# Mixing slots: low halves ahead of angle reductions, one result and one low half ahead of the last flips

## The chip, the cores and the metric

The kernel runs on one core of a Trainium2 chip. Its time is the device time of one execution in microseconds (us). A core has five engines that run their own instruction streams and meet only at semaphores: TensorE (PE, matmuls), VectorE (DVE), ScalarE (ACT), GpSimd (POOL) and SyncE (SP); POOL and SP mostly issue DMAs here. Each engine takes its instructions strictly in the order in which the program lists them.

## The reference

For 8 batches of 448 tokens and 12 heads of 64 features:

```
scores = cap * tanh(q k^T / 8 / cap);  attn = softmax(scores);  x = attn v      # x: 448 tokens x 768 features
theta  = x w_theta;  zr = x cos(theta);  zi = x sin(theta)
y      = w_tok_r zr + w_tok_i zi                                                # mixes tokens
u      = x + y;      out = u + max(u w_ch, 0)
```

## The kernel before, in words

Features stand on the partitions: a batch has six *feature blocks* of 128 features, numbered 0 to 5, each 448 tokens wide. Attention runs in 24 *slots* of four heads, three slots a batch. The dense work of a batch (its angles `theta`, the token mixing, the channel product) is spread over the three slots in which the attention of a later batch is computed, so that TensorE always has matmuls.

The order of the instructions is written out by hand: `PARTS` holds three strings of words, one for each kind of slot, and `run` turns each word into instructions. Every engine takes its own instructions in the order in which the words stand. `PARTS[0]` (*angle slot*) makes the angles, `PARTS[1]` (*mixing slot*) mixes the tokens, `PARTS[2]` makes the channel product. Batches 1 to 6 of the dense work use these strings; the first and the last batch have strings of their own in `OTHER`. So there are six mixing slots that follow `PARTS[1]`; they are called slots 1 to 6 here and start near 205, 310, 415, 520, 625 and 730 us.

The words that matter:

- `d4 d5`: `reduce`, L533 and L534, on DVE: the angles of blocks 4 and 5 are brought into one turn. `sc2`: `sincos` for blocks 4 and 5, on ACT: an absolute value (L542), a table load, cosine (L543), sine (L544). `r4 r5`: `rotate`, L548, on DVE: the features times cosine and sine.
- `f2 f3`, `f4 f5`: `flip`, L556, on DVE: blocks are transposed in squares of 32. `D1`, `D2`: `carry`, L567: 16 DMAs, 8 issued by SP and 8 by POOL, that complete the transposition of a pair of blocks into a tile `t`. D1 carries blocks 2 and 3, D2 blocks 4 and 5.
- `h`, `l`, `M`: each feature block goes through the mixing in two halves, a (four chunks of 128 columns) and b (three). `h` (`z_high`, L577, ACT) rounds a half to the high part `zh`; `l` (`z_low`, L584, DVE) subtracts it for the low part `zl`; `M` (`mix`, L594 to L596, PE) multiplies: for each chunk `zh` by the high weights, `zh` by the low weights, `zl` by the high weights. So M needs `zh` at its first matmul and `zl` at its third. `h0a l0a M0a` read the tile `t` of D0, blocks 2 and 3 that of D1, blocks 4 and 5 that of D2.
- `m0` (`mix_out`, L602, DVE): the mixed block 0 is read from PSUM and added to the features. The PSUM bank that it frees is the bank of M2.
- `S`, `t`, `e`: scores of the next heads on PE (L322), their tanh (L353) and exponential (L366) on ACT. `I`: `invert`, L472 and L475 on DVE and four DMAs (L479) on SP: the inverse of the sums of the softmax.
- `Pb1`, `Pa1`: L278 and L279 on DVE, high and low parts of q and k.

An `h` of a later half writes over the `zh` part of an earlier half, so it waits until the `M` of that half has ended. Each of the large tiles that D, f and z use is one of ten rooms that are handed on in order.

Of the kernel before, what the change touches and what calls it, by code (L numbers as in the profile page):

```python
# [78 lines left out]
def softcap_attn_then_spectral_mix(ctx, tc, qk2, v, cap, w_theta, w_tok, w_ch, outT):  # L79
# [527 lines left out]
    def chan_out(b, m):  # L607
# [6 lines left out]
    FRONT = "S0 t0 q0 q1 W cV0 v w0 e0 S1 t1 Ra cV1 e1 w1 S2 t2 Rb I Vr^ e2 S3 t3 V0^ w2 e3 w3 N"  # L614
    PARTS = (
# [179 lines left out]
```

## Time and profile before

| what | us |
|---|---|
| median of 3 runs | 876.16 (874.89 to 877.24) |
| the profiled execution, its own time | 876.32 |
| its span (first to last instruction) | 874.3 |
| PE busy | 856.1 (98% of the span) |
| DVE busy | 715.9 (82%) |
| ACT busy | 592.7 (68%) |
| POOL busy | 116.8 (13%) |
| granted TensorE clock, tenths of full speed | 9 (90% or more) in each of the 40 slices |

"Idle before" is time in which an engine had nothing running because its next instruction waited; the name behind the arrow is what ended that wait. In a timeline the first column is the start from the span's begin, the second the duration; rows of equal instructions that follow each other are merged (x2 and so on). Of PE rows the ends are modelled, so starts are compared with starts.

### The profile page before, as it was taken

What the parts mean: (1) busy time and instruction counts of PE and PEld (TensorE: products, weight loads), DVE (VectorE), ACT (ScalarE), POOL (GpSimd) and SP (SyncE); (2) the same over time, 40 slices, a digit from 0 to 9 for tenths busy, and PEclk for the clock granted to TensorE, in tenths of its full rate; (3) what the DMA queues carried; (4) which work ended last, traced back from release to release, by engine and by line L of the source; (5) the groups of instructions that cost most, each with busy time, mean ns of one, the idle gap of its engine ahead of it and who ended that gap; (6) DMA issues with size and microseconds to landing.
All of it is one profiled execution on the core that took longest, in us unless ns stands there. A gap on an engine that the chain in (4) does not pass through costs nothing.

```text
span 874.3 us, 13299 instructions
## 1 busy us (share of the span) xinstructions
PE 856.1 (98%) x4756; PEld 644.2 (74%) x4756; DVE 715.9 (82%) x1160; ACT 592.7 (68%) x693; POOL 116.8 (13%) x240
## 2 busy tenths in 40 slices
PE   9999999999999999999999999999999999999997
PEld 4336686876877868778687786787777876879996
DVE  5988989999788897898987898868979789785741
ACT  7898977678845786648956499555986378824420
POOL 1120332103100021001210013000130003200300
PEclk9999999999999999999999999999999999999999
DMA  8685386633422343223332414133152222310501
GB/s 312 203 305 200 92 249 207 199 106 83 139 64 74 97 115 107 83 84 98 94 87 85 126 55 128 53 94 117 53 145 78 85 85 78 102 43 27 144 9 58
DMA packets 51691, 99.74 MB, mean 114 GB/s; under 512 B 11232, under 2 KB 42208, under 8 KB 51616
## 3 DMA queue, kind: packets, MB, share of 16 engines
q1 hardware_dynamic: 38880, 58.81, 22.1%
q0 software_dynamic: 9568, 29.89, 11.1%
q10 hardware_dynamic: 3168, 10.09, 3.7%
q8 instruction: 39, 0.64, 0.3%
q14 instruction: 36, 0.29, 0.1%
HBM read 54.72 MB, written 11.01 MB: 75 GB/s over the span
## 4 chain that ended last, share of the span: by engine, by line
PE 78%; DVE 11%; ACT 7%; issue 2%; SPq 1%; DMA 1%; DVEq 0%
PE s L322 11%; PE a L424 10%; PE mx L594 7%; PE ch L503 7%; PE mx L596 7%; PE mx L595 7%; PE ch L505 7%; PE ch L504 7%; PE th L503 4%; PE th L504 4%; PE th L505 4%; DVE z L548 2%; PE r L456 2%; DVE g_row L556 2%; PE a L418 1%
## 5 line engine op out<-in xcount | busy, mean ns | idle before, releaser
L353 ACT ACTIVATE p<-s,singles 128x1792 f32<-128x1792 f32 (+1 forms) x54 | 93.3, 1729 | 101.1 <-PE s L322 100.8
L567 POOL DMA_DIRECT2D t<-g_row x160 | 79.5, 504 | 546.1 <-DVE x_row L486 161.8
L594 PE MATMUL mx<-wtk_h,zh 128*128 128x448 f32 x336 | 124.6, 371 | 6.7 <-DVE x L602 3.3
L596 PE MATMUL mx<-wtk_h,zl 128*128 128x448 f32 x336 | 123.9, 369 | 4.0 <-DVE zl L584 4.0
L595 PE MATMUL mx<-wtk_l,zh 128*128 128x448 f32 x336 | 123.3, 367 | 0.0
L366 ACT ACTIVATE p<-p,singles 128x1792 f32<-128x1792 f32 (+1 forms) x76 | 118.2, 1556 | 1.3 <-PE a L424 0.6
L503 PE MATMUL ch<-us,wch_h 128*128 128x448 f32 x288 | 107.0, 371 | 0.0
L503 PE MATMUL th<-xs,wth_h 128*128 128x448 f32 x288 | 106.7, 370 | 0.0
L504 PE MATMUL th<-xs,wth_h 128*128 128x448 f32 x288 | 105.6, 367 | 0.0
L505 PE MATMUL th<-xs,wth_l 128*128 128x448 f32 x288 | 105.6, 367 | 0.0
L505 PE MATMUL ch<-us,wch_l 128*128 128x448 f32 x288 | 105.3, 366 | 0.0
L504 PE MATMUL ch<-us,wch_h 128*128 128x448 f32 x288 | 105.2, 365 | 0.0
L424 PE MATMUL a<-p,v 128*64 128x448 f32 x492 | 101.8, 545 | 0.0
L594 PEld LDWEIGHTS mx<-wtk_h,zh 128*128 128x128 f32 x336 | 63.1, 188 | 17.9 <-ACT zh L577 8.8
L584 DVE TENSOR_TENSOR zl<-t,zh 128x512 fp32r<-128x512 f32 x88 | 52.7, 616 | 28.3 <-ACT zh L577 19.8
L424 PEld LDWEIGHTS a<-p,v 128*64 128x64 f32 x492 | 32.9, 136 | 56.5 <-issue 50.4
L596 PEld LDWEIGHTS mx<-wtk_h,zl 128*128 128x128 f32 x336 | 63.1, 188 | 12.1 <-DVE zl L584 6.6
L577 ACT CAST zh<-t 128x512 fp32r<-128x512 f32 x88 | 47.2, 560 | 31.0 <-PE mx L595 16.6
L595 PEld LDWEIGHTS mx<-wtk_l,zh 128*128 128x128 f32 x336 | 63.1, 188 | 5.4
L503 PEld LDWEIGHTS th<-xs,wth_h 128*128 128x128 f32 x288 | 54.0, 188 | 9.5 <-issue 3.1
L503 PEld LDWEIGHTS ch<-us,wch_h 128*128 128x128 f32 x288 | 54.0, 187 | 8.3 <-DVE few L472 1.5
L504 PEld LDWEIGHTS th<-xs,wth_h 128*128 128x128 f32 x288 | 54.0, 187 | 5.0 <-DVE xs L496 0.2
(596 smaller groups left out, 1648.0 us busy)
## 6 DMA issues: line engine op xcount, KB each, us to landing
v<-in_v ACTq DMA_DIRECT2D x22, 448.0 KB, 3.2
q<-in_qk SPq DMA_DIRECT2D x40, 224.0 KB, 3.2
t<-g_row SPq DMA_DIRECT2D x160, 56.0 KB, 2.4
t<-g_row POOLq DMA_DIRECT2D x160, 56.0 KB, 2.1
out_dram<-x SPq DMA_DIRECT2D x39, 224.0 KB, 1.9
k<-in_qk SPq DMA_DIRECT2D x35, 224.0 KB, 3.5
bc<-ri SPq DMA_DIRECT2D x58, 112.0 KB, 2.4
x_row<-in_qk SPq DMA_DIRECT2D x21, 224.0 KB, 2.8
```

The source lines that it names most:

```text
L322: nc.tensor.matmul(out[h][:, :S], kk[rows], qq[rows], start=m == 0, stop=m == len(products) - 1)
L353: nc.scalar.activation(pp, t[:, :m, :, :S], AF.Tanh, scale=qscale)
L366: nc.scalar.activation(pp, pp, AF.Exp, scale=cap_sb)
L424: nc.tensor.matmul(acc_of["a", s, i][h * D : (h + 1) * D, :S], vt[s][:, 6 * i + 3 * h + c, :], U[s, (i, c)][:, h, :], start=first and c == ...
L503: nc.tensor.matmul(acc[:, :S], wh[:, j, ms], t[:, 0, :], start=j == 0, stop=False)
L504: nc.tensor.matmul(acc[:, :S], wh[:, j, ms], t[:, 1, :], start=False, stop=False)
L505: nc.tensor.matmul(acc[:, :S], wl[:, j, ms], t[:, 0, :], start=False, stop=j == NJ - 1)
L567: queue.dma_start(t[32 * m : 32 * m + 32, d * S : (d + 1) * S], f[32 * d : 32 * d + 32, m * S : (m + 1) * S])
L584: nc.vector.tensor_tensor(zl, tokens(b, j)[:, c0:c1], zh.bitcast(F32), op=ALU.subtract)
L594: nc.tensor.matmul(acc[:, :S], zh, wtk_h[:, c, :], start=c == 0, stop=False)
L595: nc.tensor.matmul(acc[:, :S], zh, wtk_l[:, c, :], start=False, stop=False)
L596: nc.tensor.matmul(acc[:, :S], zl, wtk_h[:, c, :], start=False, stop=c == NC2 - 1)
```

## The change

Two of the three strings change; no instruction is added or removed. In the diff, the first pair is the end of `PARTS[0]`, the second the beginning of `PARTS[1]`:

```diff
-        " e2 T3 y3 Pa0 Pb0 q1 e3 d3 a1a a1b F1 sc1 T4 y4 T5 y5 r2 r3 f2 f3 D1 d4 d5",
-        "S0 t0 V0 h0a l0a h0b l0b W h1a Ra Rb Vr cV0 cV1 sc2 Pa1 S1 Pb1 q0 M0a l1a r4 h1b t1 M0b r5 l1b I f4 f5 D2 e0 h2a M1a l2a e1 M1b m0 h2b l2b w1"
+        " e2 T3 y3 Pa0 Pb0 q1 e3 d3 a1a a1b F1 sc1 T4 y4 T5 y5 r2 r3 f2 f3 D1",
+        "S0 t0 V0 h0a l0a h0b l0b W h1a Ra Rb Vr cV0 cV1 d4 d5 sc2 Pa1 S1 Pb1 q0 M0a l1a r4 h1b t1 M0b r5 l1b h2a I m0 l2a f4 f5 D2 e0 M1a e1 M1b h2b l2b w1"
```

The first place is DVE at the beginning of slot 4. `z_2` and `z_4` are the angle tiles of blocks 2, 3 and of blocks 4, 5; `t_0` is the tile of D0. Before:

```order
L556 STREAM_TRANSPOSE g_row<-z_2_4624 128x7x4x32 x2
L533 SCALAR_TENSOR_TENSOR z_4_4718<-z_4_4718 128x448
L534 TENSOR_SCALAR z_4_4718<-z_4_4718 128x448
L533 SCALAR_TENSOR_TENSOR z_4_4718<-z_4_4718 128x448
L534 TENSOR_SCALAR z_4_4718<-z_4_4718 128x448
L584 TENSOR_TENSOR zl_4790<-t_0_4631,zh_4789 128x512
L584 TENSOR_TENSOR zl_4790<-t_0_4631,zh_4789 128x384
L278 CAST q35h<-q_4511 128x448
```

and now, in the same place:

```order
L556 STREAM_TRANSPOSE g_row<-z_2_4624 128x7x4x32 x2
L584 TENSOR_TENSOR zl_4786<-t_0_4631,zh_4785 128x512
L584 TENSOR_TENSOR zl_4786<-t_0_4631,zh_4785 128x384
L533 SCALAR_TENSOR_TENSOR z_4_4718<-z_4_4718 128x448
L534 TENSOR_SCALAR z_4_4718<-z_4_4718 128x448
L533 SCALAR_TENSOR_TENSOR z_4_4718<-z_4_4718 128x448
L534 TENSOR_SCALAR z_4_4718<-z_4_4718 128x448
L278 CAST q35h<-q_4511 128x448
```

The two low halves of block 0 (l0a, l0b) and the four reductions (d4, d5) have changed places; what stands ahead and behind is the same.

The second place is DVE later in the same slot, from l1b on; `mx_0` is the mixed block 0, `t_1` the tile of D1. Before:

```order
L584 TENSOR_TENSOR zl_4790<-t_0_4631,zh_4789 128x384
L472 RECIPROCAL few_4870<-r_4803 32x14 x4
L475 STREAM_TRANSPOSE ri_4869<-few_4870 128x448
L556 STREAM_TRANSPOSE g_row<-z_4_4718 128x7x4x32 x2
L584 TENSOR_TENSOR zl_4790<-t_1_4746,zh_4789 128x512
L602 TENSOR_TENSOR x_0_3530<-mx_0_4841,x_0_3530 128x448
L584 TENSOR_TENSOR zl_4790<-t_1_4746,zh_4789 128x384
```

and now:

```order
L584 TENSOR_TENSOR zl_4786<-t_0_4631,zh_4785 128x384
L472 RECIPROCAL few_4871<-r_4799 32x14 x4
L475 STREAM_TRANSPOSE ri_4870<-few_4871 128x448
L602 TENSOR_TENSOR x_0_3530<-mx_0_4841,x_0_3530 128x448
L584 TENSOR_TENSOR zl_4786<-t_1_4746,zh_4785 128x512
L556 STREAM_TRANSPOSE g_row<-z_4_4718 128x7x4x32 x2
L584 TENSOR_TENSOR zl_4786<-t_1_4746,zh_4785 128x384
```

The result read m0 and the low half l2a stand ahead of the two flips f4 and f5 now, where they stood behind them.

On ACT one instruction moves: the rounding h2a, which l2a needs. `s_1` are scores, `p_0` the softmax tile. Before:

```order
L577 CAST zh_4789<-t_0_4631 128x384
L353 ACT_TABLE_LOAD
L353 ACTIVATE g_row<-s_1_4821,singles 128x1792
L366 ACTIVATE p_0_4780<-p_0_4780,singles 128x1792
L577 CAST zh_4789<-t_1_4746 128x512
L366 ACTIVATE g_row<-g_row,singles 128x1792
```

and now:

```order
L577 CAST zh_4785<-t_0_4631 128x384
L353 ACT_TABLE_LOAD
L353 ACTIVATE g_row<-s_1_4821,singles 128x1792
L577 CAST zh_4785<-t_1_4746 128x512
L366 ACTIVATE p_0_4776<-p_0_4776,singles 128x1792
L366 ACTIVATE g_row<-g_row,singles 128x1792
```

h2a has gone ahead of the exponential e0. The matmuls, the DMAs of each queue and the rooms of the tiles keep their order.

## Rows read from the trace of the kernel before

**Rows 1.** Who waited for whom, PE: us in total, times, longest.
```profile
PE mx L596 <- DVE zl L584: 4.0, 6, 0.7
```

**Rows 2.** Timeline, PE: first matmul of M2 in slots 1 to 6.
```profile
227.54 0.44 PE L594 MATMUL mx<-wtk_h,zh 128*128 128x448 f32 x1 [1.10 <-ACT zh L577]
...
332.63 0.44 PE L594 MATMUL mx<-wtk_h,zh 128*128 128x448 f32 x1 [1.26 <-DVE x L602]
...
437.21 0.44 PE L594 MATMUL mx<-wtk_h,zh 128*128 128x448 f32 x1 [1.24 <-DVE x_row L602]
...
542.51 0.44 PE L594 MATMUL mx<-wtk_h,zh 128*128 128x448 f32 x1 [0.99 <-DVE x L602]
...
647.83 0.44 PE L594 MATMUL mx<-wtk_h,zh 128*128 128x448 f32 x1 [1.09 <-DVE x_row L602]
...
753.10 0.44 PE L594 MATMUL mx<-wtk_h,zh 128*128 128x448 f32 x1 [1.07 <-DVE x L602]
```

**Rows 3.** Timeline, PE, slot 4: M0 (three rows), M1b, M4a.
```profile
529.91 0.37 PE L595 MATMUL mx<-wtk_l,zh 128*128 128x448 f32 x1
530.97 0.47 PE L596 MATMUL mx<-wtk_h,zl 128*128 128x448 f32 x1 [0.69 <-DVE zl L584]
531.27 0.36 PE L594 MATMUL mx<-wtk_h,zh 128*128 128x448 f32 x1
...
537.88 0.37 PE L596 MATMUL mx<-wtk_h,zl 128*128 128x448 f32 x1
...
551.67 0.37 PE L596 MATMUL mx<-wtk_h,zl 128*128 128x448 f32 x1
```

**Rows 4.** Timeline, DVE, slot 4: l0a and l0b, Pb1, r4 and r5, l1b, f4 and f5, l2a, m0.
```profile
530.23 1.16 DVE L584 TENSOR_TENSOR zl<-t,zh 128x512 fp32r<-128x512 f32 x2
531.30 0.39 DVE L278 CAST q35h<-q 128x448 fp32r<-128x448 f32 x1
...
534.59 2.09 DVE L548 TENSOR_TENSOR z<-z,x 128x896 f32<-128x896 f32 x2 [0.78 <-ACT z L544]
536.60 0.55 DVE L584 TENSOR_TENSOR zl<-t,zh 128x384 fp32r<-128x384 f32 x1
...
539.03 2.11 DVE L556 STREAM_TRANSPOSE g_row<-z 128x896 f32<-128x896 f32 x2
541.05 0.65 DVE L584 TENSOR_TENSOR zl<-t,zh 128x512 fp32r<-128x512 f32 x1
541.74 0.62 DVE L602 TENSOR_TENSOR x<-mx,x 128x448 f32<-128x448 f32 x1
```

**Rows 5.** Timeline, ACT: h4a in slot 2; L542 of sc2 and h4a in slot 4.
```profile
339.71 0.62 ACT L577 CAST zh<-t 128x512 fp32r<-128x512 f32 x1 [1.97 <-DMA t<-g_row]
...
530.41 0.95 ACT L542 ACTIVATE z<-z 128x896 f32<-128x896 f32 x1 [1.29 <-DVE z L534]
...
548.55 0.62 ACT L577 CAST zh<-t 128x512 fp32r<-128x512 f32 x1 [0.93 <-PE mx L594]
```

**Rows 6.** Timeline, SP: the issues of D2 in slot 4.
```profile
541.77 5.00 SPq L567 DMA_DIRECT2D t<-g_row  x8
```

**Rows 7.** DMA issues: count, KB each, median us from issue to landing.
```profile
t<-g_row SPq DMA_DIRECT2D x160, 56.0 KB, 2.4
```

**Rows 8.** Timeline, DVE: l4a and l4b in slots 1 to 6.
```profile
234.69 1.16 DVE L584 TENSOR_TENSOR zl<-t,zh 128x512 fp32r<-128x512 f32 x2 [1.99 <-ACT zh L577]
...
340.36 1.16 DVE L584 TENSOR_TENSOR zl<-t,zh 128x512 fp32r<-128x512 f32 x2 [2.74 <-DMA k<-in_qk]
...
444.31 1.16 DVE L584 TENSOR_TENSOR zl<-t,zh 128x512 fp32r<-128x512 f32 x2 [2.11 <-ACT zh L577]
...
549.20 1.16 DVE L584 TENSOR_TENSOR zl<-t,zh 128x512 fp32r<-128x512 f32 x2 [1.68 <-DMA k<-in_qk]
...
656.09 1.16 DVE L584 TENSOR_TENSOR zl<-t,zh 128x512 fp32r<-128x512 f32 x2 [3.27 <-DMA k<-in_qk]
...
760.21 1.16 DVE L584 TENSOR_TENSOR zl<-t,zh 128x512 fp32r<-128x512 f32 x2 [2.10 <-ACT zh L577]
```

## The prediction

> **What bounds the kernel now.** I read the table of waits for PE first, then the PE timeline of a mixing slot, then DVE, ACT and SP in the same window, and last the same few instructions in all six mixing slots. PE is busy for nearly the whole span, so the end moves only by what TensorE waits. Outside the start, its named waits are two, each once in every mixing slot. The first is M0's third matmul, which needs the low half l0a: 4.0 us over six slots [rows 1]. The second is M2's first matmul, 0.99 to 1.26 us a slot, 6.75 us together [rows 2]: the bank that M2 needs is freed by m0 (in slot 1 the name given is the rounding of h2b, which ended at nearly the same time). Both are waits on DVE's order: l0a stands behind d4 and d5, m0 behind f4 and f5. What the reader should look for next is what else hangs on d5 and on f5, since the change makes these two later.
>
> **The change part by part, in slot 4.**
>
> *First low halves ahead of d4 and d5.* M0's second matmul starts at 529.91 and the mixing runs at 0.207 us a matmul (531.27 to 537.88 is 32 of them), so the third could start at 530.12; it starts at 530.97, and the one behind it 0.30 later and not 0.21 [rows 3]. Now l0a is done before PE asks for it, which gives 0.94 us. The price stands on DVE: l0a and l0b take from 530.23 to 531.30 [rows 4], so d5 ends 1.07 us later. ACT's absolute value had sat idle for 1.29 us and started when d5 ended [rows 5], so sc2 starts and ends 1.07 later; DVE in turn had sat idle for 0.78 us and started r4 when sc2's sine ended [rows 4]. So r4, r5 and l1b come 1.07 us later: nothing on the way has slack to hide it.
>
> *What l1b holds up.* l1b ends at 537.15 [rows 4]. From the start of l0a to the matmul that waited for it were 0.74 us, about 0.13 beyond the low half itself, so M1b's third matmul could start at 537.28; it starts at 537.88 [rows 3], a slack of 0.6. Now l1b allows it at 538.35, while PE, 0.94 early, arrives at 536.94. The wait of 0.7 at M0 is gone and one of 1.4 stands at M1b; with the slower restart (0.09) PE is 0.56 us behind its old time there.
>
> *m0, l2a (and h2a) ahead of f4 and f5.* m0 would start when I is done, 539.03 plus 1.07, and end near 540.7 [rows 4]. PE reaches M2 at 542.51 less 0.99 plus 0.56, 542.08 [rows 2], so M2's wait goes altogether. Up to here slot 4 has gained 0.43 us, and the six slots 6.75 less 3.36, 3.4 us. h2a ahead of e0 is free: the half that it writes over belongs to M0, long done by then, and e0's first reader on DVE stands behind the low halves of block 3; without that cover it would cost one rounding, 0.6 us a slot.
>
> *What is late next: D2.* f4 and f5 now stand behind m0 (0.62) and l2a (0.69, from 541.05 to 541.74) and behind an l1b that is 1.07 late: f5 ends 2.38 us later than at 541.14 [rows 4]. D2 starts 0.63 after f5; SP needs 5.00 us for its eight issues [rows 6], and the last lands 2.4 us behind its issue [rows 7]: 541.77 plus seven eighths of 5.00 plus 2.4 is 548.5, and h4a, the first reader of that tile, starts at 548.55 [rows 5]. The name at that row is a matmul that had long been done; in slot 2 the same wait is put down to the carry itself, 1.97 us [rows 5]. So h4a and l4a sit on the carry already before the change, and they move by the full 2.38.
>
> The Trainium skill has a rule against this step: "DMA: Bandwidth & Descriptors", section "Issuing engines are not separate DMA queues", says that the time in which a sequencer starts its DMAs is usually small beside the transfers themselves. The trace disagrees here: eight issues take 5.00 us and a landing 2.4. By the rule D2 would be there some 2.4 us after 541.77, block 4 would have 4 us to spare, and the sum would end at the 3.4 us gained; this is the second rival.
>
> *The sum.* M4a's third matmul comes 9.16 us after M2's first (551.67 less 542.51) [rows 2, 3]. Now it cannot start before l4a's old start plus 2.38 plus 0.74, and restarts 0.09 slower. Taking l4a from [rows 8] and M2 from [rows 2], the six slots end later by 1.20, 1.78, 1.15, 0.74, 2.31 and 1.16 us, 8.3 together. What was gained further up is in this already: it only makes the wait at M4 longer. Slots 2 and 5 stand out: there l4a came 7.73 and 8.26 us after M2, in the other four 7.01 on average. If what held up those two carries doesn't meet them again, 2.0 us less are lost, 6.4. No row says whether it does; I take 7.6, nearer to what the trace has. Behind M4 nothing else waits: l5a and l5b move with l4a. The profiled execution took 876.32 us, 0.16 over the median of the runs; 876.32 plus 7.6 less 0.2 is 883.8 against 876.16.
>
> Unknown costs: whether l0a, right behind the flip f3, starts as promptly as d4 did (0 to 0.1 us a slot, which would add up to 0.6); and whether D2's issues, 1.3 us further behind the four DMAs of I than before, run faster or meet other loads (0.5 us a slot either way). The forecast's own range is 880 to 886.5.
>
> **The rivals.**
>
> *Both waits go and nothing takes their place.* 6 times 0.94 and 6.75 are 12.4 us: 864. For it: the two waits are the only ones that PE shows, and each is moved. Against: it needs sc2 not to hang on d5 and h4a not on f5, and both rows say that they do.
>
> *D2 has slack (faster).* The carry is ready before block 4 needs it, and the slot keeps what it has at M2: 3.4 us less, 872.8. One mechanism: h4a's wait is the buffer that it writes over, as the row of slot 4 names it (a matmul, not the carry), and then it follows PE. It decides the sign from the point where carries land on average 1.4 us before h4a starts (2.38 less the mean slack of 0.99 that the sum contains). Against: the sum of issue and landing meets h4a's start to 0.1 us, and slot 2 names the carry.
>
> *sc2 is not delayed (no change).* If the absolute value could start 1.07 earlier than I think, f5 is late by 1.31 alone. Then the slots lose 0.13, 0.71, 0.08, -0.33, 1.24 and 0.09 us: 1.9, so 878. Against: the row's 1.29 us of idle end with d5.
>
> **How the numbers follow.** Forecast 0.75, both waits gone 0.05, D2 with slack 0.12, sc2 on time 0.08. A measurement of this kernel can tell about 0.3%, 2.6 us, from no change. The two rivals that gain lie beyond that: faster 0.17. Within 0.3%: the third rival and a small tail of the forecast, 0.11. Slower 0.72. The range for 8 in 10 takes the forecast's own range and reaches down over the third rival, and up for slots that all behave like slot 5: 876 to 887.
>
> **What would show it.** Right: M0's wait for `zl` and M2's for L602 gone in all six slots; a new wait of about 1.4 us of M1b's third matmul on DVE's `zl`; L542 on ACT still released by d5, 1.07 us later; D2's first issue about 2.4 us later against M0's start; and a wait of M4's first and third matmul on `zh` and `zl`, 0.7 to 2.5 us a slot, with h4a released by the carry. PE's idle time in the mixing grows from 10.7 to about 18 us. Wrong: no wait at M4 (then the second rival), no wait at M1b (then the first or third), or waits in the channel slots, where DVE's backlog of 2.4 us would first be felt.

## The result, and the profile after

The changed kernel takes 881.5 us (881.19 to 882.98, 4 runs) against 876.5 us (874.89 to 877.24, 4 runs) of the kernel before, measured beside it: a ratio of 1.0063, interval 1.0044 to 1.0081. It is slower by 5.0 us, with 883.8 forecast. The profiled execution took 881.24 us, its span is 879.5.

The table of waits of the kernel after, PE (us in total, times, longest), answers to [rows 1]:

```profile
PE mx L596 <- DVE zl L584: 8.7, 6, 1.5
PE mx L594 <- ACT zh L577: 1.9, 5, 0.7
```

The first line stands for one wait in each of the six slots, as before, but twice as dear. The second is new at the matmul where it stands now, and the three lines of M2's waits, 6.75 us in [rows 2], are gone. Which matmuls wait is read from the timeline of PE in slot 4 (start, duration, engine, line; in brackets the idle time before it and what ended it): M0's first and third matmul, M1b's third, M2's first, M4a's first and third, to be held against [rows 2, 3].

```profile
532.93 0.47 PE L594 MATMUL mx<-wtk_h,zh 128*128 128x448 f32 x1
...
533.43 0.36 PE L596 MATMUL mx<-wtk_h,zl 128*128 128x448 f32 x1
...
541.84 0.47 PE L596 MATMUL mx<-wtk_h,zl 128*128 128x448 f32 x1 [1.52 <-DVE zl L584]
...
545.47 0.47 PE L594 MATMUL mx<-wtk_h,zh 128*128 128x448 f32 x1
...
554.61 0.48 PE L594 MATMUL mx<-wtk_h,zh 128*128 128x448 f32 x1 [0.31 <-ACT zh L577]
...
555.34 0.47 PE L596 MATMUL mx<-wtk_h,zl 128*128 128x448 f32 x1
```

M0 and M2 start without a wait; M1b and M4a wait. Behind them, the timeline of DVE in slot 4: l0a and l0b, r4 and r5, l1b, m0, f4 and f5, l4a and l4b; to be held against [rows 4, 8].

```profile
531.86 1.16 DVE L584 TENSOR_TENSOR zl<-t,zh 128x512 fp32r<-128x512 f32 x2
...
539.23 2.10 DVE L548 TENSOR_TENSOR z<-z,x 128x896 f32<-128x896 f32 x2 [1.82 <-ACT z L544]
541.24 0.55 DVE L584 TENSOR_TENSOR zl<-t,zh 128x384 fp32r<-128x384 f32 x1
...
543.58 0.62 DVE L602 TENSOR_TENSOR x<-mx,x 128x448 f32<-128x448 f32 x1
...
544.72 2.10 DVE L556 STREAM_TRANSPOSE g_row<-z 128x896 f32<-128x896 f32 x2
...
554.59 1.16 DVE L584 TENSOR_TENSOR zl<-t,zh 128x512 fp32r<-128x512 f32 x2 [2.42 <-DMA k<-in_qk]
```

DVE's idle time before r4 grew from 0.78 to 1.82 us, about the time by which l0a and l0b were moved ahead. ACT's idle time before the absolute value grew by 1.31 us, from 1.29 to 2.60, and the carry now releases h4a in slot 1 (timeline of ACT: h4a of slot 1, the absolute value of sc2 in slot 4), against [rows 5]:

```profile
236.67 0.62 ACT L577 CAST zh<-t 128x512 fp32r<-128x512 f32 x1 [1.60 <-DMA t<-g_row]
...
535.04 0.95 ACT L542 ACTIVATE z<-z 128x896 f32<-128x896 f32 x1 [2.60 <-DVE z L534]
```

Both traces have 4,756 matmuls in one order, so that their starts can be subtracted one by one. By how much PE fell behind its old time at each place, in us over the six slots, beside what the prediction said (each step is counted up to the matmul behind the named one, so that its late restart is in it; a whole slot goes from M0's first matmul to the one behind M4a's third):

| place | predicted | measured |
|---|---|---|
| M0's third matmul | -5.6 | -5.6 |
| M1b's third | +9.0 | +10.5 |
| M2's first | -6.75 | -7.0 |
| M4a's first to third | +11.0 | +5.3 |
| a whole slot, slots 1 to 6 | 1.20, 1.78, 1.15, 0.74, 2.31, 1.16 | 0.53, 0.82, 0.66, 0.45, 0.99, 0.42 |
| the mixing slots together | +7.6 | +3.9 |
| the last matmul | +7.6 | +5.1 |

(Predicted: 0.94, 1.50 and M2's waits from the prediction's steps; M4 is what is left to 7.6.) The four places add up to 3.2 us, the other 0.7 lie between them. Of the 1.2 us between the last two rows, 0.94 are there at M0 of slot 1, ahead of the first changed instruction: 0.33 arise in the first 10 us and 0.6 in the twelve score matmuls near 72 us. The changed order has no part in them. The other 0.3 fall outside the measured stretches of the slots and stay open. The traces of the experiments stand 0.03 to 0.74 us behind the kernel before at that M0.

### The profile page after: what moved, and what is told of

Same layout as the page of the kernel before. It is cut to its first block, busy times and chain, and to the rows that moved or that the text cites. A ratio compares the mean times of both kernels' runs of the same rounds, so it can differ in the third digit from the quotient of the medians.

```text
span 879.5 us, 13287 instructions
## 1 busy us (share of the span) xinstructions
PE 861.6 (98%) x4756; PEld 643.9 (73%) x4756; DVE 716.7 (81%) x1160; ACT 592.2 (67%) x693; POOL 118.1 (13%) x240
## 4 chain that ended last, share of the span: by engine, by line
PE 86%; ACT 5%; SPq 4%; DMA 2%; issue 1%; DVE 1%; ACTq 0%; POOL 0%; POOLq 0%
PE a L424 13%; PE s L322 13%; PE th L503 7%; PE ch L503 7%; PE th L504 7%; PE th L505 7%; PE ch L505 7%; PE ch L504 7%; PE mx L596 5%; PE mx L594 5%; PE mx L595 5%; SPq L567 4%; PE a L418 2%; PE r L456 2%; DMA t<-g_row 2%
## 5 line engine op out<-in xcount | busy, mean ns | idle before, releaser
L567 POOL DMA_DIRECT2D t<-g_row x160 | 80.7, 516 | 551.6 <-DVE x_row L486 159.2
L503 PEld LDWEIGHTS th<-xs,wth_h 128*128 128x128 f32 x288 | 54.0, 188 | 9.6 <-issue 3.1
L505 PEld LDWEIGHTS ch<-us,wch_l 128*128 128x128 f32 x288 | 54.0, 188 | 4.9
```

The lines of the kernel that those rows point to most:

```text
L503: nc.tensor.matmul(acc[:, :S], wh[:, j, ms], t[:, 0, :], start=j == 0, stop=False)
L505: nc.tensor.matmul(acc[:, :S], wl[:, j, ms], t[:, 0, :], start=False, stop=j == NJ - 1)
L567: queue.dma_start(t[32 * m : 32 * m + 32, d * S : (d + 1) * S], f[32 * d : 32 * d + 32, m * S : (m + 1) * S])
```

## The experiments

Each was timed in five rounds beside the kernel before, whose median was 876.0, 875.8 and 875.7 us in the three groups, and 876.5 beside the changed kernel: a difference between runs of two groups is uncertain by up to 0.8 us. The words of the diffs are those of `PARTS`; of each string only the stretch that differs is shown.

### Each move alone

The first move alone (second half of the change undone):

```diff
-M0b r5 l1b h2a I m0 l2a f4 f5 D2 e0 M1a e1 M1b h2b l2b w1
+M0b r5 l1b I f4 f5 D2 e0 h2a M1a l2a e1 M1b m0 h2b l2b w1
```

> The first move alone: d4 and d5 behind l0a and l0b, the rest in the old order. My theory (d5 late makes sc2 late, sc2 makes r4, r5 and l1b late, f5 makes D2 late): M0's wait goes (-0.85 us a slot), M1b's third matmul waits 1.5 as in the changed kernel, m0 ends 1.07 later than before and M2's wait grows to about 1.5. D2's first issue follows f5 by about 0.6 again, since SP is still busy with I's four DMAs, and M4 does not wait, because PE is late itself. Net +1.2 a slot: 883.7 us (880.5 to 886). Rival (sc2 or l1b have slack and the first move is a gain that the second move loses): M0's wait goes and nothing comes for it, 871.5 us.

Measured: 883.65 us (883.42 to 885.05), ratio 1.0087 (1.0073 to 1.0101). Table of waits, PE:

```profile
PE mx L596 <- DVE zl L584: 8.6, 6, 1.5
PE mx L594 <- DVE x L602: 4.8, 3, 1.6
PE mx L594 <- DVE x_row L602: 3.2, 2, 1.6
PE mx L594 <- ACT zh L577: 1.5, 1, 1.5
```

The wait at M1b is the whole 8.6 us already, and M2 now waits 1.5 to 1.6 for m0 in all six slots (one of them put down to `zh`). The move that was to free M0 costs more than it frees. The rival is out by 12 us.

The second move alone (first half undone): `d4 d5` stand at the end of `PARTS[0]` again.

> The second move alone: h2a, m0 and l2a ahead of f4 and f5, d4 and d5 in their old place. My theory: M0's wait stays (0.69), no wait at M1b, M2's wait goes (-1.15 a slot), f5 ends 1.3 later but D2 starts only 0.8 later, and l4a 0.8 later takes back part of it at M4: -0.4, +0.2, -0.5, -0.9, +0.7, -0.4 us in the six slots, about -1.3 in all: 875 us (873 to 877.5). Rival (D2 has slack): the full gain at M2, 869.6 us.

Measured: 873.48 us (872.82 to 873.78), ratio 0.9968 (0.9956 to 0.998). PE's lag over a slot is -0.5, -0.2, -0.6, -0.8, +0.3 and -1.0 us. Table of waits, PE:

```profile
PE mx L596 <- DVE zl L584: 4.1, 6, 0.8
PE mx L594 <- ACT zh L577: 0.9, 2, 0.7
```

M2 gives back 7.0 us and M4 takes 3.3: PE comes to block 4 about 1 us earlier and the carry's first issue 0.2 to 1.25 us later, more than the slack that M4 had, and the gain is 2.5 us and not 7. Here the second move is a small gain. It is the first that makes the change slower.

### The chain from d5 to r4

```diff
-Vr cV0 cV1 d4 d5 sc2 Pa1 S1
+Vr cV0 cV1 G d4 d5 sc2 Pa1 S1
+            elif word == "G":
+                nc.scalar.activation(curve, quarter, AF.Sin)
```

`curve` is one column that nothing reads any more. The sine on it makes ACT load the table of sc2's cosine while it has nothing to do.

> The changed kernel with one more ACT instruction, a sine of one column ahead of the absolute value, so that the table load of sc2 (1.28 us) runs while ACT waits for d5. Nothing else moves. My theory (the chain from d5 over sc2 to r4 is what delays l1b and D2): r4 starts 1.28 earlier, M1b's wait falls from 1.5 to about 0.2, D2 starts 1.28 earlier and with it l4a, so M4 ends 1.28 earlier too: -7.7 us against the changed kernel, 873.8 us (872 to 876). Rival (l1b waits for something else, such as h1b or its place on DVE): M1b's wait stays, 881.5 us.

Measured: 873.93 us (872.51 to 875.06), ratio 0.9978 (0.9969 to 0.9987); 7.6 us less than the changed kernel. Timeline of ACT, slot 4, and the waits of PE:

```profile
528.34 1.28 ACT L711 ACT_TABLE_LOAD   x1
...
530.90 0.95 ACT L542 ACTIVATE z<-z 128x896 f32<-128x896 f32 x1 [1.07 <-DVE z L534]
531.89 1.05 ACT L543 ACTIVATE z<-z,singles 128x896 f32<-128x896 f32 x1
```

```profile
PE mx L594 <- ACT zh L577: 2.9, 6, 1.2
PE mx L596 <- DVE zl L584: 1.1, 4, 0.3
```

The cosine follows the absolute value at once, r4 comes 1.29 us earlier (5.01 us behind M0's first matmul in slot 4, 6.30 in the changed kernel), and the 8.7 us of M1b's waits have shrunk to 1.1 at most. The Trainium skill, "ScalarE: Activation LUTs", section "What ACT_TABLE_LOAD costs", gives some 2.66 us for a switch of tables, of which about 1.28 are the load and the rest a drain. Here the load alone counts, 1.28 us in its row and 1.29 in what its removal from the chain gives.

The same instruction in the kernel before:

> The kernel before with the one-column sine ahead of sc2's absolute value, nothing else. My theory: sc2 ends 1.28 earlier, r4 starts at once behind l1a, 0.78 earlier, and with it f4, f5, m0 and D2; M0's wait stays at 0.7, M2's falls from 1.1 to about 0.3, and M4, whose carry moves with it, does not wait: -0.78 a slot, 871.3 us (869.5 to 873). Rival (M2's wait hangs on the rounding h2a or on another bank, or DVE's idle time is not on the path): 876 us.

Measured: 870.1 us (870.02 to 871.07), ratio 0.9938 (0.9925 to 0.9952). The waits of PE for m0 fell to 0.7 and 0.2 us in all:

```profile
PE mx L596 <- DVE zl L584: 4.1, 6, 0.7
...
PE mx L594 <- DVE x L602: 0.7, 3, 0.4
...
PE mx L594 <- DVE x_row L602: 0.2, 1, 0.2
```

M4 did not wait, since its carry moved with PE. The gain is 1.0 us larger than forecast (5.7 us, not 4.7).

### The carry D2 and block 4

One more DVE instruction ahead of f4 in the changed kernel:

```diff
-h2a I m0 l2a f4 f5 D2
+h2a I m0 l2a l2a f4 f5 D2
```

> The changed kernel with the low half l2a computed twice (the second writes the same values), so that f4, f5 and D2 come one DVE instruction of 0.6 us later and nothing else does; M2's third matmul still finds l2a done. My theory (in the changed kernel block 4 sits on the carry D2 without slack in all six slots): M4's waits grow by 0.62 a slot, +3.7 us against the changed kernel: 885.2 us (884 to 886.5). Rival (M4's waits there are mostly PE's own, the carry has some slack): 881.5 us.

Measured: 886.52 us (884.75 to 886.69), ratio 1.0117 (1.0102 to 1.0133), 5.0 more than the changed kernel and 1.3 more than expected. PE's waits for `zh` at M4a:

```profile
PE mx L594 <- ACT zh L577: 7.2, 6, 1.5
```

They grew from 1.9 to 7.2 us; there is no slack. D2 came 0.70 to 0.82 us later and not 0.62. A further 1.2 us of the profiled run come from slot 2 alone, told below.

Two of POOL's eight DMAs of D2 given to SP, in the changed kernel:

```diff
-queue = nc.gpsimd if (b < B - 1 or i) and d >= 2 else nc.sync
+queue = nc.gpsimd if (b < B - 1 or i) and d >= 2 and not (i == 2 and 0 < b < B - 1 and d == 2 and m < 2) else nc.sync
```

> The changed kernel with two of the eight DMAs of D2 that POOL issues given to SP, which issues ten then and POOL six; the data are the same. My theory (the carry lands when SP has issued its last DMA, plus 2.4 us): SP's stretch grows from 5.0 to 6.2 us, the last landing and with it l4a come 1.24 later, +7.4 us in six slots: 889 us (887 to 890.5). Rival (the transfers themselves set the landing, and issue time is small beside them): 881.5 us.

Measured: 889.57 us (888.35 to 891.12), ratio 1.0161 (1.0147 to 1.0175). D2's issues on SP in slot 4, and h4a on ACT:

```profile
548.94 6.25 SPq L567 DMA_DIRECT2D t<-g_row  x10
```

```profile
556.98 0.62 ACT L577 CAST zh<-t 128x512 fp32r<-128x512 f32 x1 [2.73 <-DMA t<-g_row]
```

The same bytes, 8.1 us slower. Counted from M0's first matmul, h4a came 0.65 to 1.10 us later than in the changed kernel (slot 4: 556.98 less 535.00 is 21.98, and 553.94 less 532.93 was 21.01), though POOL's own last DMA landed 0.85 to 1.14 us earlier in five of the six slots: the last issue of the longer queue sets the landing. The steps are smaller than the 1.24 expected, and the slots lost 5.5 us and not 7.4. That the total fits all the same is in part luck: in the profiled run 2.4 us stand behind the last matmul, where the span runs on for 8.24 us and not 5.81, and SP's closing semaphore waits pause for 2 us. No expectation covers that. The Trainium skill's rule in "DMA: Bandwidth & Descriptors", section "Issuing engines are not separate DMA queues", that the time to start a DMA is usually small beside the DMA, does not hold for this carry, by the trace before (5.00 us of issues, 2.4 of landing) and by this run.

### Why D2 started so soon behind f5

SP's rows in slot 4 of the kernel before (the DMAs of I, ahead of those in [rows 6]) and of the kernel after:

```profile
540.12 1.23 SPq L479 DMA_DIRECT2D bc<-ri  x2
```

```profile
544.76 1.24 SPq L479 DMA_DIRECT2D bc<-ri  x2
546.95 4.98 SPq L567 DMA_DIRECT2D t<-g_row  x8
```

Before, SP is with I's DMAs until 541.35, and f5 ends at 541.14 [rows 4]; after, SP has been free since 546.00 when f5 ends at 546.82. D2's first issue followed f5 by 0.62, 0.39, 0.97, 0.63, 0.65 and 0.97 us in the six slots before, and by 0.13 or 0.14 in all six after. I's DMAs alone do not fill these distances: they end 0.21 to 0.31 us behind f5. Behind them SP works through two to six semaphore waits of L567, 0.05 to 0.09 us apart, which the trace records and the timeline leaves out; in slots 3 and 6 some 0.36 us pass between the first two. In the changed kernel all but the last two of these are done before f5 ends. In the first move alone, where f4 stands right behind I again, the distances are 0.40 to 0.97 as before. To see that it is I's DMAs, they were moved behind D2 in the kernel before (`Q` is L472, `J` the rest of I):

```diff
-l1b I f4 f5 D2 e0 h2a M1a l2a e1 M1b m0 h2b l2b w1
+l1b Q f4 f5 D2 e0 h2a M1a l2a e1 M1b m0 J h2b l2b w1
```

> The kernel before with I cut in two: its reciprocals (L472) stay, its transpose and its four DMAs on SP stand behind m0 and D2. Nothing else moves. My theory (what held D2's first issue 0.4 to 1.0 us behind f5 in the kernel before was SP, busy with I's four DMAs): the first issue now follows f5 by 0.13 in all six slots, as in the changed kernel. f5, l2a and m0 come 0.65 earlier, M2's wait falls from 1.1 to about 0.4, M4 does not wait: -0.65 a slot, 872 us (870.5 to 873.5). Rival for the lag (it belongs to D2 or to the carry's room, not to SP's queue): the lag stays 0.4 to 1.0.

Measured: 871.2 us (870.8 to 872.17), ratio 0.9949 (0.9936 to 0.9963). SP in slot 4, with f5 ending at 539.19:

```profile
539.32 4.95 SPq L567 DMA_DIRECT2D t<-g_row  x8
544.37 1.17 SPq L730 DMA_DIRECT2D x_row<-ri  x2
```

The distance is 0.13 or 0.14 us in the slots 1, 2, 4 and 5, and 0.45 in slots 3 and 6 (0.97 before), where the remaining 0.3 us lie between the last semaphore wait and the first issue. It is the same two slots that showed a pause of 0.36 us among the semaphore waits before and in the changed kernel, where it ends ahead of f5; what causes the pause is open. (L475 moved with the DMAs, so that f5 ends 0.7 to 0.8 us earlier here as well.)

### A version that beats both

The early table load; l0a alone ahead of d4; h1b ahead of sc2's cosine (`A2` is its absolute value, `cs2` cosine and sine; the code of the new words is left out); l1b, m0 and L472 in DVE's idle time before r4; l2a and the rest of I behind f5:

```diff
-h0b l0b W h1a Ra Rb Vr cV0 cV1 d4 d5 sc2 Pa1 S1 Pb1 q0 M0a l1a r4 h1b t1 M0b r5 l1b h2a I m0 l2a f4 f5 D2 e0
+h0b d4 d5 l0b W h1a Ra Rb Vr cV0 cV1 G A2 Pa1 S1 Pb1 q0 M0a l1a h1b cs2 M0b l1b m0 Q r4 r5 t1 h2a f4 f5 D2 l2a J e0
```

> A version made from the theory. The early table load of sc2; l0a alone ahead of d4 and d5; h1b ahead of sc2's cosine; l1b, m0 and the reciprocals of I (L472) ahead of r4 and r5, in DVE's idle time; l2a and the rest of I (transpose and its four DMAs) behind f5 and D2. My theory: M0's, M1b's and M2's waits all go (at most 0.1 left at M2's third matmul), DVE has no idle time before r4, f5 ends about 0.8 earlier than in the kernel before and D2 starts 1.3 earlier, so that M4 waits only in slots whose carry lands late: -1.9 us in five slots, -1.4 in one: 865.5 us (863 to 869). Rival (M4 hangs on something other than f5 and D2): M4's wait takes the gain back, about 873 us.

Measured: 865.66 us (865.18 to 865.92), ratio 0.9878 (0.9863 to 0.9893). The page's groups of the mixing matmuls (busy, mean ns, idle before) and its chain:

```profile
PE 96%; SPq 1%; ACT 1%; DMA 1%; DVE 1%; issue 0%; ACTq 0%; POOL 0%; POOLq 0%
...
L594 PE MATMUL mx<-wtk_h,zh 128*128 128x448 f32 x336 | 124.9, 372 | 0.1
L596 PE MATMUL mx<-wtk_h,zl 128*128 128x448 f32 x336 | 123.8, 369 | 0.1
```

The mixing waits for nothing any more. On DVE (slot 4: L472 under its new line, r4 and r5, f4 and f5, l2a) no idle time is left ahead of l2a:

```profile
530.33 1.03 DVE L731 RECIPROCAL few<-r 32x14 f32<-32x14 f32 x4
531.39 2.10 DVE L548 TENSOR_TENSOR z<-z,x 128x896 f32<-128x896 f32 x2
533.40 2.10 DVE L556 STREAM_TRANSPOSE g_row<-z 128x896 f32<-128x896 f32 x2
535.42 0.65 DVE L584 TENSOR_TENSOR zl<-t,zh 128x512 fp32r<-128x512 f32 x1
```

Two parts of it were taken out again. Without `G`:

> The version b2 without the early table load. My theory: r4 does not feel it, since DVE has l1b, m0 and L472 to do until then; but t1 ends 1.28 later on ACT and S2, which needs the bank that t1 reads, waits 0.5 to 0.6 a slot: +3.5 us against b2, 869.2 us (867 to 871). Rival (everything hidden): 865.7 us. Other rival (r4 and D2 come later by the full 1.28 and M4 waits): 873 us.

Measured: 870.61 us (870.42 to 871.14). PE waits:

```profile
PE s L322 <- ACT g_row L353: 2.9, 6, 0.6
PE mx L594 <- ACT p L351: 2.2, 6, 0.4
```

S2's wait was foreseen, M3's was not: ACT stays late, and t3 frees the bank of M3 late too. Both together are 5 us, the difference. With I whole and ahead of r4:

> The version b2 with I whole again, ahead of r4 and r5. My theory: r4, f5, D2 and l2a come 0.65 later; D2 still lands in time for M4a, but M2's third matmul waits 0.6 to 0.7 for l2a in each slot: +4 us against b2, 869.6 us (868 to 871). Rival (b2 has that much slack): 865.7 us.

Measured: 868.8 us (867.61 to 870.09); the wait at M2's third matmul:

```profile
PE mx L596 <- DVE zl L584: 1.8, 6, 0.4
```

It is there; PE falls back by 0.32 to 0.52 us at that matmul, where 0.6 to 0.7 were expected.

## Why the prediction was right, and where its sizes were not

- *M0's wait goes*: right, and by its size.
- *d5 later makes sc2, r4, r5 and l1b later*: right, and shown twice: the first move alone has the wait at M1b, and the early table load takes it away. The size was 1.07 and is 1.3: r4 stands 6.30 us behind M0's first matmul (539.23 less 532.93), where it stood 4.99 (534.59 less 529.60, the row below). Of the difference some 0.2 is at l0a: d4 had started 0.07 us before f3's recorded end (528.35 against 528.42), l0a starts 0.11 after it. The prediction allowed 0 to 0.1 for that.
- *M2's wait goes*: right, and by its size.
- *f5 2.38 later*: right; counted from M0's first matmul it is 2.35 to 2.38 in the six slots.
- *D2 starts 0.63 after f5*: this is the term that failed. It was read from one row and carried over, but it was the rest of I's DMAs on SP and the semaphore waits behind them, and m0 and l2a, put between I and f4, cover them. The step is 0.13, so that D2 moves by 1.52 to 2.10 us and not by 2.38: 3.4 us less over the six slots. In slots 2 and 5 the issues also took 6.15 and 6.66 us before and 4.99 and 5.57 after, 2.3 us less; the prediction had named 2.0 for these slots and took 0.7 of it. h4a, counted from M0's first matmul, moved by 1.70, 1.12, 1.86, 2.06, 0.98 and 1.62 us, 9.3 in all and not six times 2.38, 14.3. The 8.3 us of the sum less these 5.0 are 3.3; the slots lost 3.9, and the 0.6 between is open. (M4's own term fell by more, 5.7 us, since M1b's wait took 1.5 more than forecast and so left less to wait for at M4.) The run with I's DMAs moved shows the cause in full in four of six slots, and for 0.52 of 0.84 us in the other two.
- *h4a sits on the carry*: right. One more instruction ahead of f4, two more issues on SP, and the second move alone each moved M4.
- The rivals: "both waits go" fell with the first move alone, "D2 has slack" with the second move alone and the added delay, "sc2 not delayed" with the rows of L542 (1.30 us later against M0's first matmul) and the early table load.
- Some signs did not come as named. D2's first issue was 1.5 to 2.1 us later, not 2.4; the table names no wait for `zl` at M4. And PE's idle time in the mixing rose from 10.7 to 11.0 us and not to 18, although the slots lost 3.9: a wait costs more in starts than the idle time that the page shows for it, since the ends of matmuls are modelled. In slot 4 the 0.31 us shown at M4a stand for 0.88 us between M3's last matmul and the one behind M4a's third. The groups of the pages before and after:

```profile
L594 PE MATMUL mx<-wtk_h,zh 128*128 128x448 f32 x336 | 124.6, 371 | 6.7 <-DVE x L602 3.3
L596 PE MATMUL mx<-wtk_h,zl 128*128 128x448 f32 x336 | 123.9, 369 | 4.0 <-DVE zl L584 4.0
```

```profile
L596 PE MATMUL mx<-wtk_h,zl 128*128 128x448 f32 x336 | 124.7, 371 | 9.0 <-DVE zl L584 8.7
L594 PE MATMUL mx<-wtk_h,zh 128*128 128x448 f32 x336 | 125.7, 374 | 2.0 <-ACT zh L577 1.9
```

M0's first matmul in slot 4 of the kernel before:

```profile
529.60 0.47 PE L594 MATMUL mx<-wtk_h,zh 128*128 128x448 f32 x1
```

So the mechanism was right from d5 to block 4, but the slots lost only half of the 7.6 us that the forecast gave them. That the total, 5.0 us, lies closer to it owes something to luck: in this pair of traces 1.2 us of it are not lost in the slots.

## What to carry to other kernels

A wait that goes because an instruction was moved ahead is paid by whatever stood there: follow that engine's order to the next engine that depends on it, and price those steps before the gain. Look for idle time that ends with a long chain on another engine (here 1.82 us of DVE before r4); what can stand in it without the chain cost nothing here, and taking a table load out of the chain gained 5.7 us in the kernel before, more than the 5.0 us that the whole change cost. A distance read between two instructions of different engines is a fact only with its cause: ask what the second engine did until then.

## What the runs showed of the hardware

TensorE's clock fell once behind short waits. In slot 2 of the run with the added DVE instruction PE waited for M1b, ran, and waited 1.51 us for M4a; 0.7 us later its matmuls came at 0.37 us and not 0.20, nine of them. Two rows of the timeline, and the granted clock in stretches (window, length, PE busy, clock):

```profile
344.12 0.47 PE L594 MATMUL mx<-wtk_h,zh 128*128 128x448 f32 x1 [1.51 <-ACT zh L577]
...
345.23 0.58 PE L594 MATMUL mx<-wtk_h,zh 128*128 128x448 f32 x1
```

```profile
342.00:344.10 2.10, 0.61 (x4) 1.00 0.38 117
344.10:347.10 3.00, 2.93 (x9) 0.66 0.52 156
350.00:356.00 6.00, 6.00 (x36) 1.00 0.15 38
```

That is the lower level, 1.2 GHz, which the trace records from 345.1 to 348.5 us; the 0.66 of the second stretch is a mean over both levels. It cost 1.2 us beyond the wait (against the changed kernel PE was 1.14 us later by the matmul behind M4a's third, 2.38 by M0 of the next slot). None of the other profiled runs shows it, though several of their waits are 1.5 us and longer.

At a granted clock of 1.00 the matmuls of 448 columns run at either 0.200 or 0.207 us from start to start, in stretches of some microseconds to more than 60, at other places in each trace. This does not explain the drift of 1.2 us outside the slots: taken matmul by matmul, intervals that differ by less than 0.012 us between the traces before and after add up to nothing there, and to 0.5 us inside the slots. What sets the stretches is open.
